# Linear attention and MLP, two layers: products of the denominators moved to VectorE, the scaling of the queries to ScalarE, and a new order

## The chip, the core and the metric

The kernel runs on one core of a Trainium2 chip. A core has five engines, each with a queue of its own that it works through in order: TensorE (PE, the matmuls; its weight loads are shown as PEld and overlap with them), VectorE (DVE), ScalarE (ACT), GpSimd (POOL) and SyncE (SP), which here only issues DMAs. The engines meet through semaphores. The metric is the device time of one execution in microseconds (us), median of several runs.

## The reference

Two layers, each an attention block A and an MLP block B, on x of 2048 rows and 448 columns, float32:

```python
x = x + A(layernorm(x));  x = x + B(layernorm(x))      # twice, same weights

def A(x):                       # 16 heads of 28 columns
    q, k, v = split(x @ wqkv)
    pq, pk = phi(q), phi(k)     # phi(t) = (t + 1 if t > 0 else exp(t)) + 1e-6
    kv = einsum("shd,she->hde", pk, v);  z = sum over s of pk
    num = einsum("qhd,hde->qhe", pq, kv)
    den = einsum("qhd,hd->qh", pq, z) + 1e-6
    return (num / den) @ wo

def B(x):
    return gelu(x @ w1 + b1) @ w2 + b2      # 448 -> 1792 -> 448
```

## The kernel before, in words

The 2048 rows are 16 tiles of 128 rows (t = 0 to 15). Every float32 operand of a matmul is split into a high and a low part of the type fp32r, and a product is made of two or three passes. The names below are tokens: each is a small function (`@op`), and `ORDER` (lines 15 to 142) is a long text of tokens for each layer, written out by a planner. `run` (L1058) goes through the text and calls the functions; so the order of the text is, for each engine, the order of its queue. A number behind the name is the tile or piece, `:a`, `:d`, `:p` picks the engine, and `>` or `<` in front takes the operation from the next or the previous layer, so that the layers overlap.

A layer goes through these stages.

- **Start of the program** (layer 0 only). x tiles are loaded (`ld`, L516), weights of the projections in pieces (`wkld`, `wqld`, L282 to 285) and split (`wkh`, `wkl`, `wqh`, `wql`). One piece, `wkld1:a`, is issued from ACT's queue, all others from SP's. `tab` (L269) loads ACT's tables ahead of need, `hot` runs matmuls on ones.
- **Projections.** Statistics and normalisation (`a`, `ar`, `n`; `ar` is a power on POOL, L432), turning of a tile so that columns lie on partitions (`T`, or `tu` with a round trip through DRAM), splits `xh`, `xl`; then `K` and `Q`, eleven matmuls each (L624 to 629), phi of both (`ke`, `kp`, `kh`, `kl`; `qe` are two activations, L634 and L635, `qp` one DVE instruction). phi(q) goes to DRAM (`qs`) and comes back later (`pl`, L829). `G` (L698 to 702) adds up products of the normalised x and phi(k) in four PSUM banks; `za` adds phi(k) over tiles.
- **From the sums to M.** `z` (L730) sums `za` over partitions, `zb` (L736, ACT) gives the 448 sums plus a constant, the same on every partition. `kv` (L758) makes the 28x28 blocks of all heads, `mask`, `mkh`, `mkl` clean and split them, `m` (L791 to 793) multiplies by wo, giving M, split by `mh`, `ml`.
- **Queries.** For every tile: `pz` (L834) multiplies phi(q) by `zb` on **POOL**; `pd` (L839 to 842, DVE) sums each head's 28 columns, adds a constant and takes the reciprocal `rd` of 16 columns; `pm` (L847, one DVE instruction) replaces phi(q) by (phi(q) + 1e-6) times `rd` of its head, in place. Tiles 0 to 3 are then turned by PE (`pT`, L855), tiles 4 to 15 by DVE and DRAM (`pu`, `ps`, `pp`); `qh`, `ql` split them, `o` (L892 to 894) or `oc` (L903 to 907) multiplies by M, and `oa` (L913) adds the result to x.
- **MLP**, in four blocks of four tiles. `la`, `ln`, `lx` normalise, `lb` (L935, POOL) adds b2 to x, `mT` or `mu`/`ms`/`mp` turn, `yh`, `yl` split. `f` (L971 to 975, eleven matmuls of 512 columns, 14 for each block) makes one 128-column piece of the hidden layer, `g` (L988, ACT) its gelu. The second matmul goes by Strassen's seven products: `cs` (L1005, DVE) adds quarters of the hidden layer, `ch` (ACT) and `cl` (L1018, DVE) split, `cp` (L1036, L1037) multiplies by weights that were summed and split at the start (`vd` to `vs`) and are loaded by `cw`, and `cf` (L1048, DVE) adds a product into one or two quarters of x, each as two adds (the two halves of the PSUM result).

`f` and `Q` share two PSUM banks (tag `h`), so the third of them waits until `g`, or `qe` and `qp`, has read the first. `m`, `o`, `cp` share four (`acc`), `K`, `kv`, turns and `oc` two (`m`). Small tiles such as `rd` have two buffers (L182). The program keeps eight DMA semaphores, and a DMA waits until the one that had its semaphore before has landed.

In the MLP of layer 0 the projections of the next layer begin, and some tail operations of layer 0 run in layer 1.

Of the kernel before, what the change touches and what calls it, by code (L numbers as in the profile page):

```python
# [10 lines left out]
AF = mybir.ActivationFunctionType  # L11
# [135 lines left out]
def linear_attn_mlp_kernel(  # L147
# [683 lines left out]
    @op  # L831
    def pz(l, t, e):
        T["pz", l, t] = ring(e or f"W{4 if t > 3 else 4 + t % 2}", D, "pz")
        pool.tensor_tensor(T["pz", l, t], T["pq", l, t], T[l, "zb"], op=OP.mult)  # L834
# [205 lines left out]
    def cf(l, n, e):  # L1040
# [4 lines left out]
        for r, c, how in GOES[k]:  # L1045
            xs = T["x", l, 4 * b + 2 * r + j][:, c * HD:(c + 1) * HD]
            for part in (o[:, :HD], o[:, HD:]):
                dve.tensor_tensor(xs, xs, part, op=how)  # L1048
# [46 lines left out]
```

## Time and profile before

| | |
|---|---|
| median of 3 runs | 896.0 us (895.43 to 897.46) |
| profiled execution | 891.56 us |
| its span, first to last instruction | 889.8 us |
| POOL: `pz` | 32 of 1174 ns |
| DVE: `pm` | 32 of 748 ns |
| DVE: adds into x (L1048) | 384 of 384 ns |
| DMA | 194.98 MB, 219 GB/s on average |

How to read the rows that follow: a group's row gives line, engine, operation, output and inputs, shapes, count | busy time in us, mean duration of one in ns | idle time of the engine just before them, and what ended it. A row of the waits gives who waited for whom: us in total, times, the longest. A row of the timeline gives start and duration in us, engine, line, operation, count, and in brackets the idle time before it and what ended it; a row with a count over 1 runs from the first start to the last end. A row of the windows gives from and to, length, then busy time and count of PE, PEld, DVE, ACT, POOL, the granted PE clock as a share, the DMA share and GB/s. Durations of instructions that follow each other on one engine overlap somewhat: the distance of two starts is shorter than the duration.

### The profile page before, as it was taken

How to read it: one execution, taken by the hardware profiler on the slowest of the kernel's cores; microseconds unless marked ns; L12 is line 12 of the kernel's file. 1: busy time of each engine (PE TensorE's matmuls, PEld its weight loads, DVE VectorE, ACT ScalarE, POOL GpSimd, SP SyncE). 2: the span in 40 equal slices, each digit the busy share in tenths (PEclk: the TensorE clock that was granted, in tenths of full speed). 3: DMA queues.
4: the chain of work that ended last, by engine and by line, in shares of the span. 5: the costliest groups of instructions: out<-in, count | busy, mean ns of one | idle time of the engine just before them, and what ended most of it. 6: DMA issues, size and time to landing. Idle time of an engine off the chain costs nothing.

```text
span 889.8 us, 13303 instructions
## 1 busy us (share of the span) xinstructions
PE 856.8 (96%) x4413; PEld 755.8 (85%) x4413; DVE 701.0 (79%) x1485; ACT 507.0 (57%) x1025; POOL 206.2 (23%) x249
## 2 busy tenths in 40 slices
PE   6999989999999999999999999999999989999997
PEld 5888969888888887888999899978888878888887
DVE  4777689889878967887998766866997897587588
ACT  4988764566356445744568766755635543653343
POOL 2566455221112002011113234431212020120000
PEclk8999999999999999999999999999999999999999
DMA  6555979897786945764755656275587566566545
GB/s 196 158 199 153 314 227 319 274 351 239 268 277 222 336 148 207 221 247 176 281 182 184 196 163 244 73 234 183 190 273 253 176 242 212 184 228 211 176 166 183
DMA packets 79013, 194.98 MB, mean 219 GB/s; under 512 B 9824, under 2 KB 67040, under 8 KB 71776
## 3 DMA queue, kind: packets, MB, share of 16 engines
q1 hardware_dynamic: 78800, 193.89, 65.0%
q8 instruction: 35, 0.57, 0.3%
q14 instruction: 34, 0.28, 0.1%
q10 hardware_dynamic: 144, 0.23, 0.1%
HBM read 145.56 MB, written 45.32 MB: 215 GB/s over the span
## 4 chain that ended last, share of the span: by engine, by line
PE 63%; DVE 15%; ACT 7%; DMA 5%; issue 4%; POOL 4%; SPq 1%; DVEq 0%; ACTq 0%; POOLq 0%
PE cp L1036 14%; PE cp L1037 7%; PE hp L971 7%; PE hp L973 7%; PE hp L972 7%; DVE cl L1018 3%; DVE x L1048 3%; DVE g L1005 2%; PE hp L974 2%; PE hp L975 2%; PE op L905 1%; PE op L903 1%; PE op L904 1%; PE psk L626 1%; PE G L699 1%
## 5 line engine op out<-in xcount | busy, mean ns | idle before, releaser
L1036 PE MATMUL cp<-w2s,ch 128*128 128x448 f32 x784 | 252.2, 374 | 2.1 <-DVE x L1048 2.1
L1037 PE MATMUL cp<-w2s,cl 128*128 128x224 f32 x784 | 210.0, 268 | 8.8 <-DVE cl L1018 8.6
L247 ACT CAST ch<-g 128x512 fp32r<-128x512 f32 (+1 forms) x224 | 123.1, 564 | 142.0 <-PE cp L1036 127.8
L1018 DVE TENSOR_TENSOR cl<-g,ch 128x512 fp32r<-128x512 f32 (+1 forms) x224 | 143.0, 660 | 55.6 <-ACT ch L247 52.3
L1037 PEld LDWEIGHTS cp<-w2s,cl 128*128 128x128 f32 x784 | 149.3, 190 | 18.7 <-DVE cl L1018 15.4
L1036 PEld LDWEIGHTS cp<-w2s,ch 128*128 128x128 f32 x784 | 147.2, 188 | 15.2 <-issue 2.5
L1048 DVE TENSOR_TENSOR x<-x,cp 128x224 f32<-128x224 f32 x384 | 139.3, 384 | 20.6 <-PE cp L1037 13.9
L988 ACT ACTIVATE g<-hp,b1s 128x512 f32<-128x512 f32 x112 | 76.0, 686 | 111.5 <-PE hp L975 90.5
L971 PE MATMUL hp<-XH,w1h 128*128 128x512 f32 x336 | 132.6, 395 | 0.0
L973 PE MATMUL hp<-XL,w1h 128*128 128x512 f32 x336 | 131.6, 392 | 0.0
L972 PE MATMUL hp<-XH,w1l 128*128 128x512 f32 x336 | 131.0, 390 | 0.0
L432 POOL TENSOR_TENSOR brs<-bve,mhalf 128x1 f32<-128x1 f32 x64 | 39.0, 612 | 297.7 <-ACT bve L421 196.9
L1005 DVE TENSOR_TENSOR g<-g 128x512 f32<-128x512 f32 (+1 forms) x112 | 68.1, 619 | 9.3 <-ACT g L988 8.9
L973 PEld LDWEIGHTS hp<-XL,w1h 128*128 128x128 f32 x336 | 63.0, 188 | 14.4
L971 PEld LDWEIGHTS hp<-XH,w1h 128*128 128x128 f32 x336 | 63.1, 188 | 11.9 <-ACT g L988 0.5
L972 PEld LDWEIGHTS hp<-XH,w1l 128*128 128x128 f32 x336 | 63.3, 188 | 10.8
L834 POOL TENSOR_TENSOR pz<-pq,zb 128x448 f32<-128x448 f32 x32 | 37.4, 1174 | 137.3 <-DVE dn L839 93.4
L616 POOL TENSOR_TENSOR xnl<-x,xnh 128x384 fp32r<-128x384 f32 x32 | 32.6, 1019 | 82.3 <-ACT xnh L247 70.7
L935 POOL TENSOR_TENSOR x<-x,b2b 128x448 f32<-128x448 f32 x32 | 42.6, 1342 | 35.2 <-ACT xm L441 30.1
L974 PE MATMUL hp<-XH,w1x 128*128 128x512 f32 x112 | 43.7, 390 | 0.0
L975 PE MATMUL hp<-XL,w1x 128*128 128x512 f32 x112 | 43.6, 389 | 0.0
L1005 DVE TENSOR_TENSOR g<-g,g 128x512 f32<-128x512 f32 x48 | 37.5, 785 | 5.4 <-ACT g L988 4.9
(187 smaller groups left out, 1672.2 us busy)
## 6 DMA issues: line engine op xcount, KB each, us to landing
w2s<-w_d SPq DMA_DIRECT2D x56, 1568.0 KB, 7.6
w_d<-w2o SPq DMA_DIRECT2D x7, 1568.0 KB, 7.8
x<-in_A_x_dram SPq DMA_DIRECT2D x32, 224.0 KB, 4.0
pq_d<-eq SPq DMA_DIRECT2D x32, 224.0 KB, 3.2
pq<-pq_d SPq DMA_DIRECT2D x32, 224.0 KB, 4.1
x<-x_d SPq DMA_DIRECT2D x32, 224.0 KB, 4.3
sq_a<-sq SPq DMA_DIRECT2D x13, 512.0 KB, 3.0
sp<-sq_a SPq DMA_DIRECT2D x52, 128.0 KB, 3.2
```

Source lines behind the costliest of these rows:

```text
L247: act.copy(out, src)
L971: pe.matmul(o, w1h[:, c, s], x.moving(x.hi, c), start=(c == 0), stop=False)
L972: pe.matmul(o, w1l[:, c, s], x.moving(x.hi, c), start=False, stop=False)
L973: pe.matmul(o, w1h[:, c, s], x.moving(x.lo, c), start=False, stop=False)
L974: pe.matmul(o, w1x[:, s], x.moving(x.hi, 3), start=False, stop=False)
L975: pe.matmul(o, w1x[:, s], x.moving(x.lo, 3), start=False, stop=True)
L988: act.activation(gview(l, i // KC, i % KC)[:, 0], T[l, "hp", n], AF.Gelu_apprx_tanh, bias=b1s[:, i:i + 1])
L1005: ENG[e or "d"].tensor_tensor(to, x, y, op=how)
L1018: ENG[e or "d"].tensor_tensor(lo, sums(l, n), f(hi), op=OP.subtract)
L1036: pe.matmul(o, hi[:, c, rows(j)], w[:, i], start=(i == 0), stop=False)
L1037: pe.matmul(o[:, HD:], lo[:, c, rows(j)], w[:, i, :HD], start=False, stop=(i == KC - 1))
L1048: dve.tensor_tensor(xs, xs, part, op=how)
```

## The change

- `pz` runs on DVE instead of POOL.
- `pm` is cut into two halves for each tile (tokens `pm0` to `pm31` in each layer), of eight heads each, and runs on ACT: for every head one activation of 128x28, in place, whose scale is the head's column of `rd` and whose bias is the same column times 1e-6 (`rb`, one `mul` of 16 columns for each tile). A flag `:d` would keep a half on DVE.
- `cf` goes over the halves of the product outside and over its targets inside, so that two adds that follow each other go to different places where there are two targets (80 of 112 calls).
- `wkld1` is issued from SP's queue like the other pieces; no DMA is left on ACT's queue.
- Both order texts are new from the first token to the last. But for the points above they hold the same operations, with the same engine flags; some go to the other layer's text with `>` or `<`. The program begins with `ld0`, and the first product is now `Q0`, with the loads of the `wq` pieces ahead of `wkld1`.

```diff
     @op
     def pz(l, t, e):
-        T["pz", l, t] = ring(e or f"W{4 if t > 3 else 4 + t % 2}", D, "pz")
-        pool.tensor_tensor(T["pz", l, t], T["pq", l, t], T[l, "zb"], op=OP.mult)
+        T["pz", l, t] = ring(f"W{4 if t > 3 else 4 + t % 2}", D, "pz")
+        ENG[e or "d"].tensor_tensor(T["pz", l, t], T["pq", l, t], T[l, "zb"], op=OP.mult)
...
     @op
-    def pm(l, t, e):
+    def pm(l, n, e):
+
+        t, h = divmod(n, 2)
+        heads = slice(h * H // 2, (h + 1) * H // 2)
         p3 = T["pq", l, t].rearrange("p (h d) -> p h d", d=DH)
-        dve.scalar_tensor_tensor(p3, p3, 1e-6, T["rd", l, t][:, :, None].to_broadcast([128, H, DH]),
-                                 op0=OP.add, op1=OP.mult)
+        rd = T["rd", l, t]
+        if e == "d":
+            dve.scalar_tensor_tensor(p3[:, heads], p3[:, heads], 1e-6,
+                                     rd[:, heads, None].to_broadcast([128, H // 2, DH]), op0=OP.add, op1=OP.mult)
+            return
+        if ("rb", l, t) not in T:
+            T["rb", l, t] = small(H, "rb")
+            act.mul(T["rb", l, t], rd, 1e-6)
+        for i in range(heads.start, heads.stop):
+            act.activation(p3[:, i], p3[:, i], AF.Identity, bias=T["rb", l, t][:, i:i + 1], scale=rd[:, i:i + 1])
...
-        for r, c, how in GOES[k]:
-            xs = T["x", l, 4 * b + 2 * r + j][:, c * HD:(c + 1) * HD]
-            for part in (o[:, :HD], o[:, HD:]):
+        for part in (o[:, :HD], o[:, HD:]):
+            for r, c, how in GOES[k]:
+                xs = T["x", l, 4 * b + 2 * r + j][:, c * HD:(c + 1) * HD]
                 dve.tensor_tensor(xs, xs, part, op=how)
```

The new order of layer 1 from `z` to `oc7`, as ACT and PE see it (tokens of the other engines left out):

```text
ACT: zb gt0 oh1 oh3 oh0 qe9 pm2 pm3 pm0 pm1 mkh0 qe11 qe8 qh1 mh2 mh3 mh0 mh1 qh0 pm6 qe10
     pm7 pm4 pm5 la0 qh3 qh2 la1 ln0 qe12 ln1 la3 yh0 ln3 la2 qe13 yh3 ln2 yh1 qe15 yh2 qe14
     g1 pm10 g0 ch0 pm8 pm9 pm11 g3 g2 ch1 g4 pm12 pm13 g6 ch3 pm14 pm15 qh4 qh5 g8 pm16 g5
     ch2 pm17 la4 g7 ch4 pm18 ch5 pm19 qh6 qh7
PE:  z Q9 kv Q11 Q8 pT1 m0 m2 m3 pT0 m1 Q10 o0 pT3 o1 pT2 Q12 o3 mT0 o2 mT1 Q13 mT3 Q15 mT2
     Q14 f1 f0 f3 f2 cp0 f4 f6 f8 f5 cp1 oc4 f7 cp2 cp3 oc5 cp4 f9 oc7
```

245 rows, old and new, of the table ORDER are left out of this document.

## The prediction

> **What bounds the kernel now.** I read the page's busy shares first, then TensorE's waits, then the groups by line and form, then the timeline of a few stretches, and last the busy time of each engine in the two stretches where the change puts its new work.
>
> ```profile
> PE 856.8 (96%) x4413; PEld 755.8 (85%) x4413; DVE 701.0 (79%) x1485; ACT 507.0 (57%) x1025; POOL 206.2 (23%) x249
> ```
>
> TensorE (PE) is busy for 856.8 of 889.8 us; its matmuls are untouched. So the most that a change of the other engines can win is the rest, 33 us, and what it can lose has no such bound. The waits that make up most of the 33 us:
>
> ```profile
> PE cp L1037 <- DVE cl L1018: 8.6, 13, 2.1
> PE tp L546 <- ACT tail L247: 6.8, 1, 6.8
> PE mp L793 <- DVE kvl L773: 3.4, 1, 3.4
> PE cp L1036 <- DVE x L1048: 2.1, 2, 1.1
> ```
>
> ScalarE (ACT) appears only once, in the start. With 57% it looks like the engine with room, but that is an average. The scaling of queries can begin only after `zb`, and its first tiles are wanted at once, so the room that counts is that between `z` and the first MLP blocks. The next two rows are those stretches: layer 1 from `z` to the first matmul of `oc7`, layer 0 from `z` to the end of the tenth `f`.
>
> ```profile
> 548.50:623.20 74.70, 73.14 (x388) 64.78 (x388) 53.03 (x110) 47.67 (x105) 25.58 (x25) 1.00 0.52 162
> 111.70:177.80 66.10, 61.26 (x315) 52.64 (x314) 59.64 (x117) 35.80 (x57) 26.88 (x26) 1.00 0.82 273
> ```
>
> Columns: length, then busy time of PE, weight loads, DVE, ACT, POOL. PE is idle for 1.6 us in the first and 4.8 us in the second; ACT has 27 and 30 us free.
>
> **The price of one scaling.** `pm` was one VectorE (DVE) instruction a tile. It becomes 16 activations of 128x28, each with a scale and a bias that are columns in SBUF, and a small `mul` for each tile; no token of the new order carries `:d`, so all 64 halves go to ACT.
>
> ```profile
> L847 DVE SCALAR_TENSOR_TENSOR pq<-pq,rd 128x448 f32<-128x448 f32 x32 | 23.9, 748 | 0.3
> L441 ACT ACTIVATE xm<-x,bnb,brs 128x448 f32<-128x448 f32 x28 | 21.4, 763 | 0.9
> L420 ACT ACTIVATE xm<-x,bmv 128x448 f32<-128x448 f32 x28 | 18.8, 671 | 0.9
> L418 ACT ACTIVATE x<-x 128x448 f32<-128x448 f32 x28 | 16.1, 574 | 13.0 <-DVE x L913 13.0
> L440 ACT ACTIVATE bnb<-bmv,brs 128x1 f32<-128x1 f32 x56 | 16.4, 292 | 14.5 <-POOL brs L432 12.9
> L419 ACT ACTIVATE bmv<-bmv 128x1 f32<-128x1 f32 x28 | 5.7, 203 | 0.9
> 569.86 0.57 ACT L418 ACTIVATE x<-x 128x448 f32<-128x448 f32 x1
> 571.79 0.53 ACT L634 ACTIVATE eq<-psq 128x448 f32<-128x448 f32 x1
> 572.83 0.28 ACT L440 ACTIVATE bnb<-bmv,brs 128x1 f32<-128x1 f32 x1
> 573.14 0.76 ACT L441 ACTIVATE xm<-x,bnb,brs 128x448 f32<-128x448 f32 x1
> 573.81 0.56 ACT L247 CAST XH<-tp 128x512 fp32r<-128x512 f32 x1
> ```
>
> No operand column: 203 ns for one element, 574 for 448, so (574-203)/447 = 0.83 ns an element. One column: 292 for one element. A second: 763-671 = 92 more. One head is then 292 + 92 + 27 x 0.83 = 406 ns. From one start to the next it is less: L441 took 0.76 but the cast behind it starts 0.67 later (573.14 to 573.81), so some 0.095 overlap and a head costs 0.31 us. A tile is 16 x 0.31 + 0.12 (`mul`, 203 ns and 15 elements, less the overlap) = 5.1 us, 163 us in all. The bounds: 0.20, the one-column row less its overlap, if the second column and the elements hid; 0.44, if each head waited for the one before it, as L441 does behind L440 (0.28, then 0.03). I take 0.31: it is made of rows of the same operation with the same operands, only longer.
>
> The Trainium skill, page "ScalarE: Activation LUTs", section "What ACT_TABLE_LOAD costs", states 186 ns + 0.833 ns an element, 93 ns for each column operand and 93 ns of overlap. By it a head is an estimated 302 ns, and the sums below would be about 1.3 us smaller in each stretch. Rows and page agree that the columns are paid even by a short instruction. The same page's "Rules for kernel authors" puts adds and multiplies on VectorE.
>
> **Layer 1, `z` to `oc7`.** ACT takes its queue in order. In the new order it holds, from `zb` to `qh7`, which `oc7` reads: pm0 to pm19 (160 heads, 49.6, and ten `mul`, 1.2), 8 `qe`, 5 `la`, 4 `ln`, 9 `g`, 18 casts of 512, 10 shorter copies. From the starts above `la` is 571.79-569.86 = 1.93, `qe` 572.83-571.79 = 1.04, `ln` 573.81-572.83 = 0.98.
>
> ```profile
> L988 ACT ACTIVATE g<-hp,b1s 128x512 f32<-128x512 f32 x112 | 76.0, 686 | 111.5 <-PE hp L975 90.5
> L247 ACT CAST ch<-g 128x512 fp32r<-128x512 f32 x168 | 101.9, 618 | 105.1 <-PE cp L1036 93.8 <-DVE g L1005 5.9 <-DVE x L1048 1.9
> L247 ACT CAST xnh<-x 128x448 fp32r<-128x448 f32 x32 | 17.6, 560 | 4.6 <-PE G L702 3.8 <-PE cp L1036 0.8
> ```
>
> Less the overlap, `g` is 0.59, a long cast 0.52, a short one 0.47. Sum: 50.8 + 8.3 + 9.7 + 3.9 + 5.3 + 9.4 + 4.7 = 92.1 us. PE's queue in the same stretch is 73.1 us busy in the row above; the new order has one `Q` more (2.3) and two `cp` less (2.5, both worked out below) there: 72.9. `oc7` stands in PE's queue, so PE can't be past it before ACT is: at least 92.1 - 72.9 = 19.2 us of waiting, where there were 1.6. **+17.6.** The wait does not come at one place: `pT3`, `pT2`, then `f4`, `f5` and `oc4` each stand behind `pm` halves, because a PSUM bank of `f` comes free only by its `g`, and `g` is queued behind three halves (7.5 us) while PE has one `f` and a few products to do.
>
> **Layer 0, `z` to the tenth `f`.** Up to `g8`, whose bank `f10` needs: 128 heads and eight `mul` (40.6), 7 `qe` (7.3), 8 `g` (4.7), 8 long casts (4.2), 14 short (6.6) and four `vh`:
>
> ```profile
> L247 ACT CAST w2o<-w2o 128x1568 fp32r<-128x1568 f32 x7 | 10.5, 1502 | 5.0 <-DMA x<-in_A_x_dram 2.8 <-DVE w2o L394 1.5 <-POOL w2o L394 0.5
> ```
>
> 5.7, together 69.1. PE: 61.3 busy in the row above, less one `G` that the new order has ahead of `z`. Eleven matmuls of that size take 21.09-18.82 = 2.3:
>
> ```profile
> 18.82 0.37 PE L624 MATMUL psq<-wq,XH 128*128 128x448 f32 x1
> 21.09 0.37 PE L574 MATMUL psk<-wk,XH 128*128 128x448 f32 x1
> ```
>
> So 59.0, and at least 10.1 us of waiting where there were 4.8: **+5.3.** To both I add **+2** for what sums leave out: ACT in turn waits for PE's results when PE stands, and the granted clock can fall, as it did after the idle start:
>
> ```profile
> 14.00:16.00 2.00, 1.82 (x7) 1.69 (x7) 1.57 (x4) 2.00 (x7) 0.32 (x1) 0.50 1.02 332
> ```
>
> Between 0 and 8 for this.
>
> **The later halves.** Some 24 halves lie behind those stretches.
>
> ```profile
> 401.19 0.40 PE L971 MATMUL hp<-XH,w1h 128*128 128x512 f32 x1
> 403.74 0.36 PE L1036 MATMUL cp<-w2s,ch 128*128 128x448 f32 x1
> 404.99 0.37 PE L1036 MATMUL cp<-w2s,ch 128*128 128x448 f32 x1
> ```
>
> An `f` takes 403.74-401.19 = 2.55, a `cp` of eight matmuls 1.25 and one of four half of it. Where three halves stand together (pm20, pm22, pm21 ahead of `g19` in layer 0: 7.5 us and the `g`, 8.1, while PE has cp19, f18, cp22, cp23, 5.0 us, until f16 wants that bank) they cost up to 3 us, alone nothing, since ACT has room there. **+4.5**, between 0 and 15. A new wait on DVE stands here too: `rd` has two buffers, so `pd` waits for the scaling of two tiles ago, with `cl` queued behind it.
>
> **DVE and POOL.** `pm` leaves DVE, 23.9 us by its row; `pz` comes from POOL, nearest row a product of two SBUF tiles:
>
> ```profile
> L725 DVE TENSOR_TENSOR zal<-za,zah 128x448 fp32r<-128x448 f32 x2 | 1.3, 626 | 0.8 <-ACT zah L247 0.8
> L834 POOL TENSOR_TENSOR pz<-pq,zb 128x448 f32<-128x448 f32 x32 | 37.4, 1174 | 137.3 <-DVE dn L839 93.4 <-DMA pq<-pq_d 37.0 <-ACT zb L736 3.9
> 117.16 1.53 DVE L394 TENSOR_TENSOR w2o<-w2o 128x224 f32<-128x224 f32 x5
> 821.74 1.52 DVE L1048 TENSOR_TENSOR x<-x,cp 128x224 f32<-128x224 f32 x4
> 119.25 3.37 POOL L785 TENSOR_TENSOR wol<-wot,woh 112x448 fp32r<-112x448 f32 x3 [2.63 <-issue]
> 116.78 0.17 DVE L840 TENSOR_TENSOR dn<-dn,dc 128x16 f32<-128x16 f32 x1
> 120.73 4.09 DVE L840 TENSOR_TENSOR dn<-dn,dc 128x16 f32<-128x16 f32 x1
> 122.58 2.21 POOL L834 TENSOR_TENSOR pz<-pq,zb 128x448 f32<-128x448 f32 x2
> ```
>
> 32 x 0.626 = 20.0, so that exchange is a draw. The adds into `x`: four take 1.52 when each second one needs the one before, five independent ones of that size 1.53; four in alternation take about 1.30, for 80 calls with two targets 18 us off DVE. And a DVE add of 16 columns, 0.17 us alone, took 4.09 while POOL ran `wol` and `pz`; it held up `kvl`, the 3.4 us wait of PE. The Trainium skill, page "SBUF — State Buffer", section "SBUF: two separate sides", calls the port pair of VectorE and GpSimd an exclusive lock, held for a whole instruction, for VectorE operations with two SBUF inputs. By it `pz` on DVE can itself be held by POOL's `lb`; by the row, 37.4 us of such holds leave POOL. Off the path, DVE's relief is free; on it, it can win no more than the `cl` and `x` waits of PE, 10.7 us. **-6**, between 0 and -10.7.
>
> **The start.**
>
> ```profile
> 8.47 0.37 ACTq L282 DMA_DIRECT2D stg<-in_A_wqkv_dram  x1
> 8.87 1.28 ACT L269 ACT_TABLE_LOAD   x1 [6.58 <-DMA stg<-in_A_wqkv_dram]
> 14.18 0.47 PE L546 MATMUL tp<-ident,tail 128*128 128x128 f32 x1 [6.76 <-ACT tail L247]
> ```
>
> The weight load on ACT's queue waited for another load and held ACT for 6.6 us, its table load and casts behind it, and PE's transposes behind these. On SP's queue, behind the query weights, it holds nobody there; next late are the last pieces of weights and then ACT itself, busy for 71.9 of the 86.9 us up to `z`:
>
> ```profile
> 24.80:111.70 86.90, 84.95 (x419) 76.72 (x418) 63.88 (x132) 71.89 (x149) 51.03 (x71) 1.00 0.69 212
> ```
>
> I take **-5** of the 6.8, between 0 and -8. The last adds win 0.2. The other moves of the order I cost at nothing: PE is busy for 85.0 of these 86.9 us, and what hides the moved steps is its queue.
>
> **Sum**, against the profiled execution (span 889.8, time 891.56): 17.6 + 5.3 + 2 + 4.5 - 6 - 5 - 0.2 = +18.2, a time of 909.8. The median of the runs shown is 896.0, 4.4 above the profiled one, so 914.2; I forecast 914.
>
> **Rivals.** *A head is cheap (faster).* If the column operands of short activations hide and a head costs 0.20, layer 1's queue falls by 160 x 0.11 = 17.6 to 74.5 and layer 0's by 14.1 to 55.0: ACT is no bound, the 4.8 us of layer 0 go as well, the later halves cost 1, layer 1 keeps its 1.6, and the sum is -4.8 + 1 - 6 - 5 - 0.2 = -15.0: 881. It decides from about 0.25 down, where the sum is zero (each 0.01 is worth 2.9 us in the stretches and 0.3 later). For it: no row has two columns and few elements; ACT's 43% idle. Against: 292 against 203 ns at one element shows that a column is paid at small size. Chance 0.2.
> *Heads in series (slower still).* In-place slices of one tile that wait for each other cost 0.44 each: 288 x 0.13 = 37 more and some 10 in the later halves, 962. Against: different columns. Chance 0.05.
> *Even.* A head at 0.25, between those two prices: 896. Chance 0.04.
>
> **How the numbers follow.** The forecast has 0.71; the ends of its terms give 900 and 942, which won't all fall together, so its own range is 902 to 930. The range 886 to 931 leaves out most of the cheap head, the series and the upper corner. 0.2% is 1.8 us, about what a measurement of this kernel tells from no change. Faster 0.20, same 0.04, slower 0.76.
>
> **What would show it.** Right: 512 activations that write `pq`, of about 0.41 us, starting 0.31 apart; ACT nearly 670 us busy and full in the stretches behind each `z`; PE waits for `g`, `ch`, `qh` behind ACT of some 15 to 20 us in layer 1 and 10 in layer 0; first idle of PE shorter by 5 us; the x adds 0.3 apart. Wrong: heads 0.2 apart, or PE's idle behind `z` as small as before.

## The result, and the profile after

| | before | after |
|---|---|---|
| median | 896.73 us (895.43 to 897.88, 4 runs) | 943.14 us (940.57 to 944.55, 4 runs) |
| ratio to before | | 1.0515, 95% interval 1.0487 to 1.0543 |
| span of the profiled execution | 889.8 us | 941.3 us |
| mean granted PE clock in it | 0.995 | 0.982 |

The change makes the kernel 46.4 us slower. The forecast had the direction and the mechanism (PE waits behind ACT's queue), but +18 in place of +46, and the time lies above its range. The two profiled spans differ by 51.5 us, since the profiled execution of before lies some 5 us below its median; the parts below add up to these 51.5.

The busy line of the page of after:

```profile
PE 881.0 (94%) x4413; PEld 764.2 (81%) x4413; DVE 670.7 (71%) x1485; ACT 663.2 (70%) x1571; POOL 166.8 (18%) x217
```

ACT has 156 us more (507.0 before), DVE 30 and POOL 39 less: the work went where the change sends it. PE executes the same 4413 matmuls, yet is busy for 24 us longer and idle for 27 us more (60.3 against 33.0). So two things have to be explained, waits and slower matmuls.

The groups of after for the new work (line, engine, operation, shapes, count, then busy us and mean ns):

```profile
L860 ACT ACTIVATE pq<-pq,rb,rd 128x28 f32<-128x28 f32 x512 | 159.6, 397 | 1.1
L835 DVE TENSOR_TENSOR pz<-pq,zb 128x448 f32<-128x448 f32 x32 | 20.3, 636 | 0.0
L841 DVE TENSOR_TENSOR dn<-dn,dc 128x16 f32<-128x16 f32 x32 | 7.1, 222 | 1.2
```

A head lasts 397 ns (the forecast: 406). The short add L841, which POOL held up before, is down from 345 to 222 ns.

PE's waits in after (who waited for whom: us in total, times, longest):

```profile
PE hp L983 <- ACT g L1000: 14.3, 9, 5.2
PE tq L867 <- ACT pq L860: 10.8, 11, 1.4
PE cp L1048 <- ACT ch L248: 7.9, 7, 2.4
PE cp L1049 <- DVE cl L1030: 6.7, 14, 3.0
PE mp L792 <- ACT kvh L248: 4.9, 2, 4.4
PE op L915 <- ACT qh L248: 4.0, 2, 2.1
```

Five of the six are for ACT, 41.9 us, and only one of these (`tq`, the turn of scaled queries) is for a scaled tile. The others are for ordinary steps (`g`, `ch`, `kvh`, `qh`) which stand behind scaling in ACT's queue. The wait for the tail in the start, 6.8 us, is gone.

The program in four stretches, cut at `z` of layer 0, the end of the tenth `f`, `z` of layer 1 and the first matmul of `oc7`; columns as in the prediction. Of before, the two stretches that the prediction didn't show:

```profile
177.80:548.50 370.70, 363.79 (x1885) 323.01 (x1884) 299.50 (x648) 213.71 (x438) 67.94 (x82) 1.00 0.68 233
623.20:889.70 266.50, 257.09 (x1349) 224.93 (x1348) 214.62 (x456) 124.91 (x251) 28.82 (x27) 1.00 0.60 208
```

and all four of after:

```profile
104.90:186.60 81.70, 66.05 (x303) 53.55 (x301) 53.31 (x114) 70.40 (x188) 17.50 (x15) 0.94 0.68 230
186.60:569.70 383.10, 368.92 (x1874) 323.83 (x1875) 288.40 (x648) 250.32 (x574) 56.66 (x74) 0.99 0.64 217
569.70:670.10 100.40, 81.74 (x383) 68.20 (x382) 49.18 (x106) 93.50 (x266) 10.68 (x12) 0.93 0.35 116
670.10:941.20 271.10, 261.24 (x1364) 227.06 (x1364) 202.59 (x461) 157.73 (x365) 21.89 (x24) 1.00 0.61 213
```

| stretch | before | after | difference | at equal work |
|---|---|---|---|---|
| start to `z`, layer 0 | 111.7 | 104.9 | -6.8 | -9.1 |
| `z` to tenth `f`, layer 0 | 66.1 | 81.7 | +15.6 | +17.9 |
| to `z`, layer 1 | 370.7 | 383.1 | +12.4 | +12.4 |
| `z` to `oc7`, layer 1 | 74.7 | 100.4 | +25.7 | +25.7 |
| to the end | 266.5 | 271.1 | +4.6 | +4.6 |

(The column "at equal work" moves the one `G`, 2.3 us, that stood behind `z` before and stands ahead of it now.) The sum is 51.5. ACT is the fullest engine in the two stretches behind a `z`, 70.4 of 81.7 and 93.5 of 100.4 us, and PE's clock is lowest there, 0.94 and 0.93.

The sums of ACT's queue were close: 69.1 was forecast and 70.4 is measured, 92.1 and 93.5. But ACT isn't busy throughout. It is idle for 11.3 and 6.9 us, and its waits in the first and in the second stretch say why:

```profile
ACT eq L635 <- PE psq L630: 4.3, 3, 1.7
ACT g L1000 <- PE hp L987: 3.2, 1, 3.2
ACT XH L248 <- PE tp L472: 2.3, 1, 2.3
```

```profile
ACT g L1000 <- PE hp L987: 2.2, 1, 2.2
ACT Mh L248 <- PE mp L794: 1.6, 2, 1.0
ACT eq L635 <- PE psq L630: 1.0, 1, 1.0
```

ACT waits for PE, which waits for ACT. One place shows how, the timeline of ACT and PE around `f5` and `f4` of layer 0 (start, duration, engine, line, in brackets the wait; rows between these are left out):

```profile
160.30 2.51 ACT L860 ACTIVATE pq<-pq,rb,rd 128x28 f32<-128x28 f32 x8
162.71 0.20 ACT L858 ACTIVATE rb<-rd 128x16 f32<-128x16 f32 x1
162.95 4.92 ACT L860 ACTIVATE pq<-pq,rb,rd 128x28 f32<-128x28 f32 x16
167.78 0.66 ACT L1000 ACTIVATE g<-hp,b1s 128x512 f32<-128x512 f32 x1
168.50 0.79 PE L983 MATMUL hp<-XH,w1h 128*128 128x512 f32 x1 [5.21 <-ACT g L1000]
170.37 0.63 PE L984 MATMUL hp<-XH,w1l 128*128 128x512 f32 x1
174.49 0.39 PE L983 MATMUL hp<-XH,w1h 128*128 128x512 f32 x1
```

Sixteen heads last 4.92 us, 15 steps of 0.30 and the last head's 0.40. The `g` of 0.66 us, which frees the PSUM bank, stands behind three halves; PE waits 5.21 us for it. Then its matmuls last 0.63 us, and from 174.5 on 0.39: the granted clock in the windows around it is

```profile
168.00:170.00 2.00, 1.50 (x4) 1.22 (x5) 1.00 (x4) 2.00 (x3) 0.00 (x0) 0.50 0.15 61
170.00:172.00 2.00, 2.00 (x6) 1.59 (x5) 2.00 (x2) 0.42 (x1) 0.00 (x0) 0.50 0.51 205
```

It is 0.50 for 6.8 us (167.5 to 174.3). In the second of these windows ACT is idle in its turn, 0.42 busy of 2.00 us: PE is slow now, and the next `g` isn't there. Counted over the trace, PE has 35.2 us at half clock in after, of it 24 in the two stretches behind a `z` (spells of 3.4 or 6.8 us), and 10.2 in before, all of it at the start and the end (1 us of the one and 2 of the other lie behind the last instruction). The Trainium skill, page "TensorE: Matmul & The Clock Gate", section "Part 1: The HAM clock gate", has the clock fall to half after an idle window of about 3.4 us and rise after a busy one, with windows that run freely. The spells' lengths, one and two times 3.4, agree, and so do their starts: those at 167.5 and 256.3 us are 26 times 3.41 us apart. The wait that it takes is another matter. That 3.4 us of waiting for `kvl` in before brought no spell fits windows that run freely. But in after two short waits some 3 us apart, of 1.3 and 1.1 us (ending at 341.8 and 345.0), brought one, and no 3.4 us there are idle throughout; here the trace differs from the page.

### The profile page after: what moved, and what is told of

It reads as the page before. It is cut to its first block, busy times and chain, and to the rows that moved or that the text cites. A ratio compares the mean times of both kernels' runs of the same rounds, so it can differ in the third digit from the quotient of the medians.

```text
span 941.3 us, 13786 instructions
## 1 busy us (share of the span) xinstructions
PE 881.0 (94%) x4413; PEld 764.2 (81%) x4413; DVE 670.7 (71%) x1485; ACT 663.2 (70%) x1571; POOL 166.8 (18%) x217
## 5 line engine op out<-in xcount | busy, mean ns | idle before, releaser
L1048 PE MATMUL cp<-w2s,ch 128*128 128x448 f32 x784 | 255.3, 376 | 10.4 <-ACT ch L248 7.9
L1030 DVE TENSOR_TENSOR cl<-g,ch 128x512 fp32r<-128x512 f32 (+1 forms) x224 | 138.7, 638 | 75.3 <-ACT ch L248 74.5
L860 ACT ACTIVATE pq<-pq,rb,rd 128x28 f32<-128x28 f32 x512 | 159.6, 397 | 1.1
L983 PE MATMUL hp<-XH,w1h 128*128 128x512 f32 x336 | 136.0, 405 | 14.3 <-ACT g L1000 14.3
L985 PE MATMUL hp<-XL,w1h 128*128 128x512 f32 x336 | 133.9, 398 | 0.5 <-DVE XL L508 0.3
L1060 DVE TENSOR_TENSOR x<-x,cp 128x224 f32<-128x224 f32 x384 | 124.6, 380 | 10.6 <-PE cp L1049 9.3
L1017 DVE TENSOR_TENSOR g<-g 128x512 f32<-128x512 f32 (+1 forms) x112 | 65.3, 592 | 13.0 <-ACT g L1000 12.4
L947 POOL TENSOR_TENSOR x<-x,b2b 128x448 f32<-128x448 f32 x32 | 40.0, 1263 | 23.1 <-ACT xm L442 22.9
L480 DVE STREAM_TRANSPOSE sq<-pq 128x384 f32<-128x384 f32 x24 | 13.7, 570 | 38.8 <-ACT pq L860 38.8
L1017 DVE TENSOR_TENSOR g<-g,g 128x512 f32<-128x512 f32 x48 | 33.3, 700 | 10.1 <-ACT g L1000 9.8
```

The lines of the kernel that those rows point to most:

```text
L860: act.activation(p3[:, i], p3[:, i], AF.Identity, bias=T["rb", l, t][:, i:i + 1], scale=rd[:, i:i + 1])
L983: pe.matmul(o, w1h[:, c, s], x.moving(x.hi, c), start=(c == 0), stop=False)
L985: pe.matmul(o, w1h[:, c, s], x.moving(x.lo, c), start=False, stop=False)
L1017: ENG[e or "d"].tensor_tensor(to, x, y, op=how)
L1030: ENG[e or "d"].tensor_tensor(lo, sums(l, n), f(hi), op=OP.subtract)
L1048: pe.matmul(o, hi[:, c, rows(j)], w[:, i], start=(i == 0), stop=False)
```

## The experiments

Two theories. **The queue**: ACT's queue behind each `z` is longer than PE's, and its excess, with what it sets off, is the loss. **The order**: the new orders of PE and DVE lose by themselves. The other parts of the change get a run each. Medians are device times, ratios go to the kernel before on the same chip.

**e1: the scaling back on DVE, all else as in after.** Every token `pmN` becomes `pmN:d` in both texts:

```diff
-        "... oh1 pd0 pm0 pz2 "
+        "... oh1 pd0 pm0:d pz2 "
```

> The kernel after with all 64 halves of the scaling on VectorE and everything else kept. Theory Q (ScalarE's queue behind z is over-full with the head activations): the waits for g, qh, ch, pq behind ScalarE go, the start keeps its gain of some 10 us: 885 us, between 878 and 893. Rival O (the new orders of TensorE and VectorE cost time by themselves): 925 us or more, with TensorE's waits moved to VectorE.

880.44 us, ratio 0.981 (0.9774 to 0.9845). The page, and the only wait of PE over 2.5 us:

```profile
PE 856.9 (98%) x4413; PEld 755.5 (86%) x4413; DVE 693.6 (79%) x1549; ACT 508.2 (58%) x1027; POOL 165.4 (19%) x217
```

```profile
PE psq L625 <- DVE eq L640: 2.9, 1, 2.9
```

PE's busy time is back at 856.9. So the scaling on ACT costs 62.7 us in this order, and all the rest of the change wins 16: the order theory falls.

**e2 and e3: part of the scaling back on DVE.** `:d` for pm0 to pm19 of each layer (e2), and for pm20 to pm31 (e3).

```diff
-        "... cp22 cs18 pm20 pm22 pm21 g19 ..."
+        "... cp22 cs18 pm20:d pm22:d pm21:d g19 ..."
```

(e3; in e2 the edit is that of e1, up to pm19.)

> The kernel after with the halves pm0 to pm19 on VectorE, pm20 to pm31 left on ScalarE. Q: the lag that builds up behind each z (18.6 us in layer 0, 27 in layer 1) goes, the 15 us that the later halves cost in layer 0 stay: 900 us, between 890 and 908. O: 930 or more. If the sum of this gain and that of the late halves alone is over the gain of all, they share waits.

> The kernel after with the halves pm20 to pm31 on VectorE, pm0 to pm19 left on ScalarE. Q: only the loss of layer 0 between TensorE's 160 and 300 us of work (15 us) and 2 us of layer 1 go: 926 us, between 920 and 932. O: 940 or more.

e2: 900.35, ratio 1.004 (1.0019 to 1.0061), 42.8 less than after. e3: 926.9, ratio 1.033 (1.0293 to 1.0367), 16.2 less. The two gains add up to 59.0 of 62.7. The longest wait of after stays in e3:

```profile
PE hp L983 <- ACT g L1000: 11.0, 7, 5.3
```

Two thirds of the loss come from the halves close behind `z`, as the queue theory says. But the later halves, for which the forecast had 4.5, cost 16.

**e4: the scaling on ACT in the old order.** The kernel before with the new `pm`, each `pmN` replaced by `pm2N pm2N+1` in its place:

```diff
-        "... ol0 pz0 pd0 va3:d oh1 oh2 pm0 Q9 vh3 ..."
+        "... ol0 pz0 pd0 va3:d oh1 oh2 pm0 pm1 Q9 vh3 ..."
```

> The kernel before, its order kept, with the scaling alone on ScalarE, both halves of a tile at the place of the old token. Q: some 155 us more on ScalarE in an order that was not made for it: 940 us, between 920 and 965, TensorE waiting for g, ch and qh behind ScalarE. O: 900 us or less, since ScalarE has 40% free.

1014.87, ratio 1.1312 (1.1275 to 1.135), mean clock 0.951, that is some 100 us at half clock. The expectation is missed by 75 us, in the same direction as the forecast of the change. The waits of PE:

```profile
PE hp L982 <- ACT g L999: 22.7, 9, 5.2
PE cp L1047 <- ACT ch L247: 18.3, 7, 8.7
PE cp L1048 <- DVE cl L1029: 18.0, 20, 6.6
```

The scaling on ACT costs 118 us in the old order, against 62.7 in the new one. With a comparable amount of work on ACT (667.5 us busy, 663.2 in after) the time is 72 us above that of after; the other parts of the change (e6 to e8 below) make up some 19 of these if they add up. So a good part of the loss is set by where the halves stand between ACT's other steps. A sum of the queue's work alone can't give it.

**e5: PE kept busy in four long waits.** After, with matmuls on ones put ahead of `f5` and `f16` in layer 0 and of `m0` and `cp0` in layer 1:

```diff
-        "... pd7 g0 f5 g5 ..."
+        "... pd7 g0 hot20 f5 g5 ..."
```

(the others: `hot14`, `hot16:acc`, `hot10`)

> The kernel after with idle matmuls on ones (20, 14, 16 and 10 of them) put into TensorE's queue right ahead of its four longest waits, so that it is not idle there; they are extra work, and nothing else changes. If the spells at half clock that follow those waits cost time of their own: four spells (23.9 us at half clock) go and 6 to 11 us are won, 934 us. If ScalarE's queue sets the time anyway and TensorE catches up for nothing: 943 us, as after.

937.21, ratio 1.0448 (1.0417 to 1.0479): 6 us faster than after. The wait for `g` and the clock in the same place:

```profile
PE hp L983 <- ACT g L1000: 8.1, 10, 2.3
```

```profile
170.00:172.00 2.00, 2.00 (x11) 1.65 (x10) 1.97 (x3) 1.09 (x3) 0.00 (x0) 1.00 0.34 135
```

Eleven matmuls in 2 us in place of six. The half clock falls from 35.2 to 20.0 us. 15.2 us at half clock do the work of 7.6, so 7.6 was to be had and 6 came. The clock is a part of the loss, not most of it: by this rate, as an estimate, the 25 us more that after has are some 10 us. Of the 24 us by which PE is busy longer in after, up to 25 / 2 = 12.5 are slower matmuls; the rest isn't separated.

**e6, e7, e8: the other parts, each alone in the kernel before.** e6 issues `wkld1` from SP; e7 exchanges the loops of `cf`; e8 puts `pz` on DVE.

```diff
-        "ld1 hot16 a1 ar1 ld0 a0 wkld0 tab0 wkld1:a tab1 ..."
+        "ld1 hot16 a1 ar1 ld0 a0 wkld0 tab0 wkld1 tab1 ..."
...
-        for r, c, how in GOES[k]:
-            xs = T["x", l, 4 * b + 2 * r + j][:, c * HD:(c + 1) * HD]
-            for part in (o[:, :HD], o[:, HD:]):
+        for part in (o[:, :HD], o[:, HD:]):
+            for r, c, how in GOES[k]:
+                xs = T["x", l, 4 * b + 2 * r + j][:, c * HD:(c + 1) * HD]
...
-        pool.tensor_tensor(T["pz", l, t], T["pq", l, t], T[l, "zb"], op=OP.mult)
+        ENG[e or "d"].tensor_tensor(T["pz", l, t], T["pq", l, t], T[l, "zb"], op=OP.mult)
```

> The kernel before with one token changed: the second key weight piece is loaded from SP's queue. If the 10 us that the changed kernel wins up to z come from freeing ScalarE's queue: 891 us, 5 to 6 less than before, the wait for the tail copy gone. If they come from the new order of loads and products at the start: 896 us, within 1.5.

> The kernel before with only the loops of the adds into x exchanged. The adds get some 0.1 us closer where they needed each other, 15 to 18 us off VectorE in all. If VectorE's relief reaches the path: 893 us, 2 to 5 less. If the order has hidden them: 896 us.

> The kernel before with only the denominators' products on VectorE. 20 us of work come to VectorE, and the holds by GpSimd's products go (7.6 us of longer VectorE instructions, and the 3.4 us wait for kvl). If the holds weigh more: 893 us. If the added work weighs more: 899 us or above, in waits for cl.

e6: 888.47, ratio 0.9913 (0.9889 to 0.9937). e7: 889.7, 0.9929 (0.9903 to 0.9954). e8: 892.25, 0.9967 (0.9947 to 0.9986). The gains of e6 and e7 are above what was expected. Together the three win 18.7 us, where e1, which has all three and the new order, is 16.1 us faster than before: if the three add up, the order itself, without scaling on ACT, wins nothing (e10 below, with the order and the parts of e6 and e7, is 9.4 us faster, where these two alone give 14.6). In e6 ACT's table load begins at 2.31 us in place of 8.87, and PE turns the tail at 8.34 in place of 14.18:

```profile
2.31 1.28 ACT L269 ACT_TABLE_LOAD   x1
8.34 0.27 PE L546 MATMUL tp<-ident,tail 128*128 128x128 f32 x1
```

In e7 PE's waits for `cl` fall from 8.6 to 6.6 (4.9 in the row and one of 1.7 at L1036), in e8 that for `kvl` from 3.4 to 1.1:

```profile
PE cp L1037 <- DVE cl L1018: 4.9, 8, 2.1
```

```profile
PE mp L793 <- DVE kvl L773: 1.1, 1, 1.1
```

**e9: a quarter of the activations.** After, with one activation for four heads; it scales all four by the reciprocal of the first, which is not what the reference computes:

```diff
-        for i in range(heads.start, heads.stop):
-            act.activation(p3[:, i], p3[:, i], AF.Identity, bias=T["rb", l, t][:, i:i + 1], scale=rd[:, i:i + 1])
+        for i in range(heads.start, heads.stop, 4):
+            act.activation(p3[:, i:i + 4], p3[:, i:i + 4], AF.Identity, bias=T["rb", l, t][:, i:i + 1], scale=rd[:, i:i + 1])
```

> The kernel after with one activation for four heads of 28 columns (112 elements), which uses the first head's reciprocal for all four, so the scaling is computed otherwise than in the reference; 4 in place of 16 instructions a tile. By the measured head (0.30 us a start, 0.023 of it elements) one takes 0.37, a tile 1.5 in place of 4.8 us. If ScalarE's queue is the cause, layer 1's queue up to qh7 falls from 91 to about 58 us, under TensorE's 73: 886 us, between 880 and 895. If something else in the new place of the scaling costs (its semaphores, the two buffers of the reciprocals): 915 or more.

869.13, ratio 0.9717 (0.9678 to 0.9756), 11 us below the range that was expected. The page:

```profile
PE 852.8 (98%) x4413; PEld 754.0 (87%) x4413; DVE 667.0 (77%) x1485; ACT 560.7 (65%) x1187; POOL 167.2 (19%) x217
```

Same order, same place of the work, same release of DVE, and 74 us less than after for 103 us less work on ACT. It is also 11 us faster than e1 (8 by the ratios). The two differ in where `pm` runs, so this is most likely what taking `pm` off DVE is worth where it costs ACT little. In after this gain can't be seen.

**e10: e1 with `pz` on POOL.** Every `pzN` of e1 becomes `pzN:p`:

```diff
-        "... ld8 pz0 oh0 ol0 db oh1 pd0 pm0:d pz2 "
+        "... ld8 pz0:p oh0 ol0 db oh1 pd0 pm0:d pz2:p "
```

> The kernel after with the scaling on VectorE and the products back on GpSimd: only the new order, the alternating adds and the load on SP's queue are left of the change. If the products' move to VectorE is a gain by itself: 884 us or more, against 880 with it. If it is a loss: 877 or less.

886.0, ratio 0.9901 (0.9873 to 0.9929): 5.6 us slower than e1, so `pz` on DVE is a gain in the new order too (4.1 in the old one).

**e11 and e12: half of the halves, and a mixture.** e11 gives `:d` to the odd halves of all tiles; e12 to pm0 to pm19 and to the odd ones behind them.

```diff
-        "mask mkh pm1 pd2 pm4 mkl ..."
+        "mask mkh pm1:d pd2 pm4 mkl ..."
```

(e11; in e12 both carry `:d`.)

> The kernel after with every odd half of the scaling on VectorE and every even one on ScalarE: half of the activations, in every tile. If the loss is a threshold (ScalarE's queue against TensorE's in the same stretch): layer 1's queue up to qh7 is 25 + 41 = 66 us against 73 of TensorE, so nearly the whole loss goes: 885 us, between 878 and 892. If the loss is in proportion to the activations: 911 us, half way from 880 to 943.

> The kernel after with pm0 to pm19 on VectorE and of pm20 to pm31 only the even halves on ScalarE, where ScalarE has room. If the later halves cost where two or three stand together and nothing alone: 880 us, no more than the kernel with all on VectorE, perhaps 2 less since VectorE has less to do. If each costs in proportion: 890 us, half way to the 900 with all of them on ScalarE.

e11: 885.61, ratio 0.9895 (0.9876 to 0.9914). In proportion, half of the 62.7 us would be left, 911.8; 5 are left (8 by the ratios). Its waits for `g`:

```profile
PE hp L983 <- ACT g L1000: 3.1, 5, 1.3
```

The loss is not in proportion to the heads. With 80 heads less in layer 1's stretch, ACT's queue there is some 67 us by the forecast's prices and PE's 72.9, so a threshold would explain it. But e11 also makes every bunch of halves shorter, and the two weren't separated. e12: 882.17, ratio 0.9866 (0.9844 to 0.9887). In proportion, its later halves on ACT would cost half of the 20 us between e1 and e2; they cost 1.7 by the medians and 5 by the ratios. This speaks for halves that cost most where two or three stand together. No version that keeps heads on ACT one at a time beats e1, which beats both kernels.

## Why the forecast had the sign right and the size wrong

- **Where the 33 us are missing.** Forecast were +18.2, measured 51.5 between the spans. At equal work the two stretches behind a `z` have 17.9 + 25.7 = 43.6, where the forecast had 5.3 + 17.6 + 2 = 24.9; the two others have 17.0, where it had 4.5 - 6 - 0.2 = -1.7; the start has -9.1, where it had -5. So the forecast is short in two places, by some 19 us each.
- **The price of a head held.** 397 ns and 0.30 from start to start, against 406 and 0.31; the cheap head and the heads in series are out. The trace's distance is (4.92 - 0.40) / 15 = 0.301. The estimate of 302 ns from the figures of the Trainium skill (page "ScalarE: Activation LUTs", section "What ACT_TABLE_LOAD costs") agrees with it.
- **The bounds of the two stretches held as bounds.** ACT's busy time is 1.3 and 1.4 us above the sums. Ten `mul`, `qe`, `g` and casts were priced rightly from before's rows.
- **The step that failed is the "+2 for what sums leave out".** It took the stretch to be as long as ACT's queue, with ACT all but always busy. Measured lengths exceed the forecast queues by 81.7 - 69.1 = 12.6 and 100.4 - 92.1 = 8.3, together 20.9 in place of 2; 18.2 of them are ACT's idle time, and 14.6 of that are the rows of its waits above, which end on a product of PE (9.8 in layer 0 and 4.8 in layer 1). Two queues that wait for each other lose in both: halves in a bunch let PE stand, then PE's late results let ACT stand. In layer 0, for example, PE waits for scaled tiles until 136.7 us and then works without such a wait, and ACT stands four times for its results between 142 and 153 us. The sum took the longer queue of the whole stretch, but which queue is the later one changes within it. The half clock behind PE's waits makes the second part larger; by e5's rate the clock's share in the whole program is some 10 us. How the rest divides between the bunches and the clock wasn't separated.
- **The later halves, +4.5, were the second mis-sized term.** e3 gives 16.2 (the upper bound was 15), and the stretches there 12.4 and 4.6 more than before, with DVE's relief in them. There are 28 such halves, 64 less the 20 and 16 of the two stretches, and not some 24; e3 has 24 of them. The place that the forecast named is right: three halves ahead of `g19` in layer 0, which it put at up to 3 us, cost a wait of 3.68, and the clock falls behind it. ACT, and the waiting `f16`, in the timeline:

```profile
251.35 4.93 ACT L860 ACTIVATE pq<-pq,rb,rd 128x28 f32<-128x28 f32 x16
256.18 0.66 ACT L1000 ACTIVATE g<-hp,b1s 128x512 f32<-128x512 f32 x1
256.90 0.80 PE L983 MATMUL hp<-XH,w1h 128*128 128x512 f32 x1 [3.68 <-ACT g L1000]
```

  The forecast priced the wait and not the 6.8 us at half clock that follow.
- **The start, -5, was too small.** At equal work it is -9.1, and e6 alone gives -7.9. "Next late" was ACT itself by the forecast; but ACT's table load and casts simply moved ahead with it.
- **DVE and POOL, -6, can't be seen in after.** e7 and e8 alone give -6.7 and -4.1 in the kernel before, and e9 suggests some 10 us for `pm` off DVE, so where ACT is not in the way the relief is larger than forecast. In after PE waits for ACT, and no run shows how much of it is left.
- The adds in alternation behave as forecast: four take 1.27 us in after (1.30 was forecast, 1.52 before). The worry that POOL's `lb` would hold `pz` on DVE didn't come: 636 ns on average, against 626 of the row it was priced by.

## What to carry to other kernels

Where work moves to an engine with an in-order queue, sum that queue over the stretch in which the work must be done, not over the program: the sum is a lower bound of the stretch, and here it gave the sign. Two engines that feed each other lose more than the longer queue, because each of them also waits for the other's late results; here ACT was idle for a tenth of the two stretches in which it was the fullest engine. With half of the heads on ACT (e11) little of the loss was left. Look at what stands behind a bunch of small instructions, for it is the short `g` or cast behind it that costs, and price a PE wait of some 4 us with the half clock that can follow it.

## What the runs showed of the hardware

- A wait of PE of 3.7 to 5.2 us was followed by half clock for 6.8 us in after. Matmuls on ones in the wait took it away (e5: clock 1.00 in place of 0.50 at 170 us).
- One DMA on ACT's queue held ACT for 6.6 us, since it had to wait for another load to land; issued from SP the same load held nobody that mattered, and 7.9 us were won (e6).
- Adds into the same place one behind the other cost DVE more than alternating ones: 1.52 against 1.27 us for four. 384 adds are 139 us busy before and 125 in after; the time won by it alone, 6.7 us (e7), is half of that.
